# Turning the second norm's rows with VectorE and DRAM instead of TensorE, tile by tile, in a one-core transformer block

## The chip, the core and the metric

The kernel runs on one core of a Trainium2 chip. A core has five engines with a queue of instructions each, which run side by side and wait for each other through semaphores: TensorE (PE in the profile; its weight loads are PEld), VectorE (DVE), ScalarE (ACT), GpSimd (POOL) and SyncE (SP), which here issues nearly all the DMA transfers. [...] PSUM, where TensorE leaves its results, is used in eight banks of 128 rows by 512 f32 numbers. The metric is the device time of one execution in microseconds (us); the median of three runs before the change is 1670.11 us (1667.31 to 1671.17).

## The reference

One block with conditioning: a norm, attention with 32 query heads over one shared key and value head, a second norm, and two dense layers with ReLU. All is f32; x has 2048 rows of 512.

```python
mod = (_silu(c) @ w_mod).reshape(1, 6, 1, -1)
sa, ca, ga, sb, cb, gb = (mod[:, i] for i in range(6))
h = _layernorm(x) * (1 + ca) + sa
x = x + ga * attention(h)          # wq, wk, wv, wo; 32 heads of 16, one key/value head
h = _layernorm(x) * (1 + cb) + sb  # the second norm
x = x + gb * (relu(h @ w1) @ w2)   # 512 -> 1792 -> 512
```

The change concerns the second norm: its result `h` stands with rows of x on the partitions, and the first dense layer needs it turned, with the 512 features on the partitions.

## The kernel before, in words

The 2048 rows are worked in eight blocks of 256 (`TB`), each of two tiles of 128 rows (`TT`). After a start of some 115 us (first norm, keys, values, first queries) comes the main loop of 256 passes, called **steps** here: 32 steps to a block. A step has two parts, one per key tile of 128 keys. In a step TensorE computes 8 score tiles (`ps_exp`, L753, three banks), 8 tiles of scores for the row maxima of a later group of heads (`ps_max`, L426, three banks), and, at the end of each part, the products with the values (`ps_pv`, L879, one bank). ScalarE takes the exponential of each `ps_exp` tile (L755), VectorE the maximum over each `ps_max` tile (L428); each of them so gives a bank back to TensorE.

Between these, in a fixed order written as two strings (`PARTS`, a letter for each instruction or small group: c and d are scores, a and b maxima, u and l the two halves of other work), TensorE does other work from a generator: `behind(b)` hands out, one portion for each step, the output projection, second norm and dense layers of the block whose attention was finished last. A portion is mostly 6 or 12 products, each done as two halves of 64 rows (`on_half`, L163). The portions of a block are: steps 1 to 3 the rest of the second dense layer of the block before; steps 4 to 7 the output projection, two steps to each tile of 128 rows; steps 8 to 14 (`fill`) the second dense layer's second tile of the block before (in the first block of this kind: queries, and products that only keep TensorE busy); steps 15 to 28 the first dense layer; steps 29 to 32 the begin of the second. There are seven such blocks in the main loop; the eighth runs after it in `behind_last`, which the change does not touch.

The generator goes on by one portion inside the last l of a step (`advance`), and whatever it emits for the other engines on the way is written there, near the end of the step. Work in the list `put_off` is written a little into the next step, after the fourth letter of part one. The softmax sums of a group of heads come every eight steps (`normalise` at the end of steps 7, 15, 23 and 31, with a VectorE reciprocal, L789, and the transfers `recs` and `den` two steps later, and a product `on`, L923, on GpSimd one step after that).

The second norm in this setting: VectorE takes the sums of a tile (`ln_sums`: L208, L209), three small VectorE operations (L220 to L222) and thirteen small GpSimd ones (L230 to L235) give the reciprocal root (`ln_stats`), and three GpSimd passes over the tile make `xn` (`normed`: L482, L484, L485). TensorE then turns `xn` in two goes of four 128x128 squares (`turned_too`, in halves by `in_two`, L159), each go into a `ps_exp` bank that it takes from the scores; ScalarE copies that bank out (`stg`, L248) and `split` makes of it a high part (`hh`, ScalarE, L240) and a low part (`hl`, GpSimd, L241), which the first dense layer reads.

Of the kernel before, what the change touches and what calls it, by code (L numbers as in the profile page):

```python
# [19 lines left out]
P = 128  # L20
# [16 lines left out]

PARTS = "cbcuaucuautcuau", "tbldlbldlbldlad"  # L40
SYNC = mybir.DependencyInfo(mybir.DependencyClass.Sync, mybir.DependencyReason.DATA)
MANUAL = {ET.PE, ET.Activation, ET.DVE, ET.Pool, ET.SP}

# [13 lines left out]
def build(tc, nc, cst, sb, ps, dr, x, wq, wk, wv, wo, w1, w2, c, w_mod, out):  # L57
# [148 lines left out]
    def ln_sums(mv, t, src):  # L206
        st = sb.tile([P, 6], F32, name="st", tag="st", bufs=2)
        nc.vector.bn_stats(st, src)  # L208
        nc.vector.bn_aggr(mv[:, t], st)  # L209

    def ln_mv(n):
        return sb.tile([P, n, 2], F32, name="mv", tag="mv", bufs=2)
# [33 lines left out]
    def split_psum(hi, lo, pt, func=AF.Copy, stg=None, **kw):  # L246
        stg = stage() if stg is None else stg
        nc.scalar.activation(stg, pt, func, **kw)  # L248

        def parts():  # L250
            split(hi, lo, stg)

        return parts


    put_off = []

    def add_psum(dst, pt, other):
        stg = stage()
# [119 lines left out]
            qps[u].append(t.rearrange("p a n -> p (a n)"))  # L379


    later, turns = [], []

    negms = [cst.tile([P, 32], F32, name=f"negm{n}") for n in range(2)]
    for negm in negms:
# [69 lines left out]
    def turned(src, k2, pt):  # L455

        return [("turn", pt[:, (k * TT + t) * P:(k * TT + t + 1) * P],
                 src[:, t, (k2 * 2 + k) * P:(k2 * 2 + k + 1) * P])
                for k in range(2) for t in range(TT)]

    def flat(t, k2):
        return t[:, k2 * 2:k2 * 2 + 2].rearrange("p a n -> p (a n)")
# [17 lines left out]
    def normed(x1, xn, ts, nm, y, eng):  # L480
        for n, t in enumerate(ts):
            eng.tensor_scalar(xn[:, t], x1[:, t], nm[:, n:n + 1], y[:, n:n + 1],  # L482
                              op0=OP.add, op1=OP.mult)
            eng.tensor_tensor(xn[:, t], xn[:, t], cbr, op=OP.mult)  # L484
            eng.tensor_tensor(xn[:, t], xn[:, t], sbr, op=OP.add)  # L485
# [25 lines left out]
    def behind(b):  # L511
        def in_parts(todo, n):
            for i in range(0, len(todo), n):
                yield todo[i:i + n]

        def turned_too(src, parts, k2, bank):

            def turn():
                pt = bank()

                def end():
                    put_off.append(split_psum(flat(parts[0], k2), flat(parts[1], k2), pt))

                return turned(src, k2, pt), end

            turns.append(turn)

        def second(b, t):
            pt = ps_fill()
            yield from in_parts(dense2(b, t, pt), 6)  # L530
            ot = sb.tile([P, D], F32, name="ot", tag="tmp", bufs=2)
            add_psum(ot, pt, x1s[b][:, t])
            nc.sync.dma_start(out[b * TB + t * P:b * TB + (t + 1) * P], ot)

        x1, oo = open_block(b)
        if b == 0:
            qqs = [sb.tile([P, 2, LB], F32R, name="qq", tag="w1s", bufs=3) for _ in range(2)]
            rest, fill = [others_of(14 + n, qqs[n]) for n in range(2)]
            fill = itertools.chain(fill, [[]] * 4)
        else:  # L540
            rest, fill = carried.pop(), second(b - 1, 1)
        yield next(rest)
        yield next(rest)
        for k2 in range(DC // 2):
            put_off.append(partial(split, flat(oo[0], k2), flat(oo[1], k2), flat(on[b], k2)))
        yield from rest
        xn = sb.tile([P, TT, D], F32, name="xn", tag="xn", bufs=1)
        mv = ln_mv(TT)
        for t in range(TT):
            pt = ps_fill()  # L550
            for n, part in enumerate(in_parts(out_proj(pt, oo, t), 6)):
                yield part
                if t and n == 0:
                    ln_sums(mv, 0, x1[:, 0])
            add_psum(x1[:, t], pt, x1[:, t])
        ahead = [load_w1(f) for f in range(2)]

        def second_norm():
            ln_sums(mv, 1, x1[:, 1])
            stats = ln_stats(mv, TT, False)  # L560
            yield
            normed(x1, xn, range(TT), *stats, nc.gpsimd)
            yield

        norm2 = second_norm()
        hp = [sb.tile([P, DC, TB], F32R, name=n, tag="t4", bufs=2) for n in ("hh", "hl")]
        for n, part in enumerate(fill):
            if n in (4, 5):
                turned_too(xn, hp, n - 4, ps_exp)
            yield part  # L570
            next(norm2, None)
        r4 = r4s[b] = [sb.tile([P, 8, TB], F32R, name="r4", tag="big", bufs=4) for _ in range(4)]
        for f2 in range(FC // 2):
            pt = ps_fill()
            for f in range(f2 * 2, f2 * 2 + 2):
                if f + 2 < FC:
                    ahead.append(load_w1(f + 2))
                yield dense1(pt[:, (f % 2) * TB:(f % 2 + 1) * TB], ahead.pop(0), hp)
            i, f = divmod(f2 * 2, 8)
            put_off.append(split_psum(  # L580
                r4[i * 2][:, f:f + 2].rearrange("p a n -> p (a n)"),
                r4[i * 2 + 1][:, f:f + 2].rearrange("p a n -> p (a n)"), pt, AF.Relu))
        first_half = second(b, 0)
        yield from itertools.islice(first_half, 4)
        carried.append(first_half)
# [206 lines left out]

        return [back, partial(nc.gpsimd.tensor_tensor, on[b][:, g], num, den, op=OP.mult)]

    def in_two(turn):

        begun = []

        def first_part():
            begun.extend(turn())  # L800
            for d in begun[0]:
                on_half(d, 1)

        def second_part():
            for d in begun[0]:
                on_half(d, 0)
            begun[1]()

        return first_part, second_part

    def run(g):
        for _ in g:
            pass
# [59 lines left out]
    def values(s):  # L873
        nonlocal pvt
        u, kt = divmod(s, KT)
        if kt == 0:
            pvt = ps.tile([P, 512], F32, name="ps_pv", tag="pv", bufs=1)
        for i in range(4):
            nc.tensor.matmul(pvt[i * 32:(i + 1) * 32], vt[:, kt], pes.pop((s, i)),  # L879
                             start=(kt == 0), stop=(kt == KT - 1))  # L880
        if kt == KT - 1:

            ends.extend((s // 2 + 2 + n, end) for n, end in enumerate(normalise(u, pvt)))

    for c in range(NU * KT // 2):
        s = c * 2
        todo_of = dict(
            c=[partial(scores, *n) for n in ((s, 0), (s, 2), (s + 1, 0), (s + 1, 2))],
            d=[partial(scores, *n) for n in ((s + 2, 1), (s + 2, 3), (s + 3, 1), (s + 3, 3))
               if n[0] < NU * KT])  # L890
        if places:
            u, i, j = places.pop(0)
            todo_of.update(a=[partial(max_of, u, 0, i, j, kb) for kb in range(KB)],
                           b=[partial(max_of, u, 1, i, j, kb) for kb in range(KB)])
        for parts, load in later:
            put_off.append(parts)
            ends.append((c, load))
        later.clear()
        if not portion:

            pt = ps_fill()
            portion = [("f32r", pt, kp[:, 0:P], kp[:, 0:512], n == 0, n == 5) for n in range(6)]
        halves = [in_two(turn) for turn in turns]
        turns.clear()
        own = []
        for h in range(2):
            each = [partial(on_half, d, h) for d in portion]
            cuts = [len(each) * k // 6 for k in range(7)]
            own.append([partial(in_turn, each[x:y]) for x, y in zip(cuts, cuts[1:])])
        own[0].append(advance)  # L910
        todo_of.update(l=[partial(in_turn, own[0][k:k + 1 + k // 5]) for k in range(6)], u=own[1])
        for part in range(2):
            todo_of["t"] = [partial(in_turn, [half[part] for half in halves])]
            for n, what in enumerate(PARTS[part]):
                if todo_of.get(what):
                    todo_of[what].pop(0)()
                if part == 0 and n == 3:
                    in_turn(put_off)
                    put_off.clear()
            values(s + part)  # L920
        for due in [end for end in ends if end[0] <= c]:
            ends.remove(due)
            due[1]()  # L923
        next(todo, None)
        if c == NU * KT // 2 - 2:
            opened = open_last(NB - 1)
        if c and c % 32 == 0:
            assert next(others, None) is None
            others = behind(c // 32 - 1)
            portion = next(others)  # L930
# [31 lines left out]
```

## Time and profile before

| what | value |
|---|---|
| median of three runs | 1670.11 us |
| the profiled execution's own time | 1670.93 us |
| its span, first to last instruction | 1669.1 us |
| mean granted TensorE clock | 0.991 |
| busy: TensorE, VectorE, ScalarE, GpSimd | 98%, 81%, 74%, 21% of the span |
| products of the turns (L159) | 112, busy 12.3 us |

The page's first part gives the busy time of each engine as a share of the span. A matmul's end is modelled, so a busy TensorE can still wait. Steps can be read off the trace: a part of a step ends with the value products (`ps_pv`, L879), so the time from the start of one step's second group of them to the next step's is the length of one step. The view by windows gives the busy time of each engine, with the number of instructions in brackets, in stretches cut at these points. Of the seven blocks that run inside the loop, the one with steps 6 to 14 between 709.65 and 763.72 us is used for the timeline.

### The profile page before, as it was taken

The numbers are of one execution on the slowest core, as the hardware profiler recorded it, in microseconds if no ns is written. First come the engines' busy times: TensorE is split into PE (matmuls) and PEld (weight loads), VectorE is DVE, ScalarE is ACT, GpSimd is POOL, SyncE is SP. The second block draws the span as 40 slices with busy tenths as digits, with TensorE's granted clock in tenths as the row PEclk, the third lists the DMA queues.
The fourth block names the chain that finished last, engine by engine and source line by source line (L and its number), as shares of the span: only waits on it lengthen the run. The fifth ranks groups of instructions, "written<-read, shape, count | busy, mean of one in ns | idle before, by whom it ended". The sixth has DMA issues, their size and how long they took to land.

```text
span 1669.1 us, 34028 instructions
## 1 busy us (share of the span) xinstructions
PE 1644.1 (98%) x13130; PEld 927.4 (56%) x13130; DVE 1354.8 (81%) x2336; ACT 1228.9 (74%) x2399; POOL 345.3 (21%) x433
## 2 busy tenths in 40 slices
PE   7999999999999999999999999999999999999999
PEld 5445555555654566545654566546654565456668
DVE  7788888888888888888888888888889888888031
ACT  4228888877877788778877788778877788778831
POOL 3102355431101311131102211131103111131110
PEclk9699999999999999999999999999999999999999
DMA  8024643312311131112301131103311131103331
GB/s 285 23 73 121 206 133 104 92 62 68 115 29 48 34 110 63 35 42 86 105 17 48 47 104 55 54 23 99 92 30 36 50 115 40 61 17 101 116 115 57
DMA packets 88080, 129.86 MB, mean 78 GB/s; under 512 B 25140, under 2 KB 52724, under 8 KB 87920
## 3 DMA queue, kind: packets, MB, share of 16 engines
q1 hardware_dynamic: 86208, 127.55, 24.6%
q8 instruction: 105, 1.72, 0.4%
q14 instruction: 55, 0.45, 0.1%
q10 hardware_dynamic: 1712, 0.13, 0.1%
HBM read 100.33 MB, written 25.15 MB: 75 GB/s over the span
## 4 chain that ended last, share of the span: by engine, by line
PE 90%; ACT 4%; DVE 3%; issue 1%; DMA 1%; POOL 0%; SPq 0%; POOLq 0%; ACTq 0%; DVEq 0%
PE ps_pv L879 29%; PE ps_exp L753 21%; PE ps_max L426 18%; PE ps_fill L163 16%; ACT pe L755 3%; PE ps_exp L146 2%; PE ps_max L146 1%; DVE pm L428 1%; PE ps_exp L307 1%; PE ps_fill L146 1%; DVE st L208 1%; PE ps_exp L293 1%; DMA wmod<-in_w_mod_dram 1%; PE ps_exp L190 1%; PE ps_exp L159 0%
## 5 line engine op out<-in xcount | busy, mean ns | idle before, releaser
L428 DVE TENSOR_REDUCE pm<-ps_max 128x1 f32<-128x512 f32 x2048 | 1273.0, 682 | 189.6 <-PE ps_max L426 173.8
L755 ACT ACTIVATE pe<-ps_exp 128x512 f32<-128x512 f32 x2048 | 1081.9, 605 | 279.6 <-PE ps_fill L163 135.2
L426 PE MATMUL ps_max<-kp,qp 48*128 48x512 f32 x2048 | 848.8, 428 | 8.5 <-DVE pm L428 8.4
L753 PE MATMUL ps_exp<-qp,kp 50*128 50x512 f32 x2048 | 766.4, 415 | 3.7 <-ACT pe L755 2.0
L879 PE MATMUL ps_pv<-pe,vt 128*32 128x512 f32 x4096 | 545.5, 605 | 0.0
L426 PEld LDWEIGHTS ps_max<-kp,qp 48*128 48x128 f32 x2048 | 373.1, 186 | 269.1 <-DVE pm L428 234.3
L753 PEld LDWEIGHTS ps_exp<-qp,kp 50*128 50x128 f32 x2048 | 360.2, 185 | 266.1 <-ACT pe L755 176.9
L163 PE MATMUL ps_fill<-w2r,r 64*128 64x512 f32 x1044 | 289.2, 405 | 0.0
L163 PE MATMUL ps_fill<-hh,w1s 64*128 64x256 f32 x1568 | 229.1, 286 | 0.0
L163 PEld LDWEIGHTS ps_fill<-hh,w1s 64*128 64x128 f32 x1568 | 204.9, 186 | 6.7 <-PEq L156 6.7
L163 PEld LDWEIGHTS ps_fill<-w2r,r 64*128 64x128 f32 x1044 | 180.9, 185 | 7.6 <-PEq L156 2.5
L879 PEld LDWEIGHTS ps_pv<-pe,vt 128*32 128x32 f32 x4096 | 80.6, 108 | 128.0 <-issue 107.6
L241 POOL TENSOR_TENSOR r<-stg,r 128x512 fp32r<-128x512 f32 x49 | 62.9, 1284 | 317.5 <-ACT r L240 317.4
L163 PE MATMUL ps_fill<-hl,w1s 64*128 64x256 f32 x784 | 126.0, 280 | 0.0
L163 PE MATMUL ps_fill<-hT,wq 64*128 64x256 f32 x416 | 118.2, 399 | 0.0
L163 PEld LDWEIGHTS ps_fill<-hl,w1s 64*128 64x128 f32 x784 | 105.5, 186 | 0.0
L163 PEld LDWEIGHTS ps_fill<-hT,wq 64*128 64x128 f32 x416 | 70.1, 185 | 2.7
L923 POOL TENSOR_TENSOR on<-num,den 128x256 f32<-128x256 f32 x31 | 22.8, 736 | 230.0 <-DMA den<-recs 203.6
L769 POOL COPY num<-pvs 128x256 f32<-128x256 f32 x32 | 12.7, 397 | 174.9 <-ACT pvs L765 174.9
L241 POOL TENSOR_TENSOR hl<-stg,hh 128x512 fp32r<-128x512 f32 x14 | 17.9, 1282 | 128.0 <-ACT hh L240 128.0
L261 POOL TENSOR_TENSOR x<-stg,x 128x512 f32<-128x512 f32 x14 | 18.1, 1292 | 97.8 <-ACT stg L260 97.8
L248 ACT ACTIVATE stg<-ps_fill 128x512 f32<-128x512 f32 x62 | 38.1, 615 | 0.0
(147 smaller groups left out, 924.1 us busy)
## 6 DMA issues: line engine op xcount, KB each, us to landing
w1s<-w1dr SPq DMA_DIRECT2D x104, 512.0 KB
qdr<-qq SPq DMA_DIRECT2D x48, 256.0 KB
qp<-qdr SPq DMA_DIRECT2D x128, 96.0 KB
raw<-in_B_w_dram SPq DMA_DIRECT2D x28, 256.0 KB
w1dr<-w1s SPq DMA_DIRECT2D x14, 512.0 KB
wmod<-in_w_mod_dram SPq DMA_DIRECT2D x6, 1024.0 KB
x<-in_A_x_dram SPq DMA_DIRECT2D x8, 512.0 KB
out_dram<-ot SPq DMA_DIRECT2D x16, 256.0 KB
```

The source lines that it names most:

```text
L146: nc.tensor.matmul(pt, w, a, start=start, stop=stop)
L163: ins = nc.tensor.matmul(pt, w[r], a[r], start=start and h == 1, stop=stop and h == 0)
L190: nc.tensor.matmul(pt, sgw[:, k], wm[i][:, k], start=k == 0, stop=k == DC - 1)
L241: (eng or nc.gpsimd).tensor_tensor(lo, src, hi.bitcast(F32), op=OP.subtract)
L248: nc.scalar.activation(stg, pt, func, **kw)
L261: nc.gpsimd.tensor_tensor(dst, stg, other, op=OP.add)
L426: nc.tensor.matmul(pt, qps[u][i][r, j * P:(j + 1) * P], kp[r, kb * 512:(kb + 1) * 512], start=True, stop=True)
L428: nc.vector.tensor_reduce(pms[u][:, (i * 2 + hf) * 4 + j, kb:kb + 1], pt, axis=AX.X, op=OP.max)
L753: nc.tensor.matmul(pt, kp[r, kt * P:(kt + 1) * P], qps[u][ct // 2][r], start=True, stop=True)
L755: nc.scalar.activation(pe, pt, AF.Exp)
L879: nc.tensor.matmul(pvt[i * 32:(i + 1) * 32], vt[:, kt], pes.pop((s, i)), start=(kt == 0), stop=(kt == KT - 1))
L923: due[1]()
```

## The change

- The sums and statistics of the two tiles are kept apart (`mvs`, one each). The chain of the first tile (`norm_of(0)`) is written at step 8, before the sums of the second are taken; the second (`norm_of(1)`) at the end of step 9.
- TensorE's turns, their `ps_exp` banks and ScalarE's copies out of these are gone, with `turned_too`, `in_two`, `turns` and the letter t.
- Instead VectorE turns each tile of 128x512 in squares of 32 by 32 (`turn_of`: one STREAM_TRANSPOSE, into `xt`), for the first tile at the end of step 9, for the second in the second part of step 11 (`half_later`). Each `xt` is written to DRAM (`xdr`) by one transfer, so that four further transfers, written at the end of step 12, bring the squares back in their final places (`xh`, one transfer for each 32 partitions, in runs of 128 numbers).
- The splits of the two halves of `hh` and `hl` then read `xh` and stand together in step 14.

```diff
-PARTS = "cbcuaucuautcuau", "tbldlbldlbldlad"
+PARTS = "cbcuaucuaucuau", "bldlbldlbldlad"
...
         xn = sb.tile([P, TT, D], F32, name="xn", tag="xn", bufs=1)
-        mv = ln_mv(TT)
+        xdr = dr.tile([32, TT, 4, D], F32, name="xdr", tag="xdr", bufs=2)
+        mvs = [ln_mv(1) for t in range(TT)]
+
+        def norm_of(t):
+            normed(x1, xn, (t,), *ln_stats(mvs[t], 1, False), nc.gpsimd)
+
+        def turn_of(t):
+            xt = sb.tile([P, D], F32, name="xt", tag="tmp", bufs=2)
+            nc.vector.transpose(xt.rearrange("p (j k n) -> p k j n", j=4, k=DC),
+                                xn[:, t].rearrange("p (k j n) -> p k j n", j=4, k=DC))
+            nc.sync.dma_start(xdr[:, t].rearrange("a i n -> i a n"), xt)
+
...
         def second_norm():
-            ln_sums(mv, 1, x1[:, 1])
-            stats = ln_stats(mv, TT, False)
-            yield
-            normed(x1, xn, range(TT), *stats, nc.gpsimd)
+            put_off.append(partial(norm_of, 0))
+            yield
+            ln_sums(mvs[1], 0, x1[:, 1])
+            yield
+            norm_of(1)
+            turn_of(0)
+            yield
+            half_later.append(partial(turn_of, 1))
+            yield
+            yield
+            xh = sb.tile([P, TT * 4, DC, 32], F32, name="xh", tag="xn", bufs=1)
+            pieces = xdr.rearrange("a t i (j m) -> j a (t i) m", j=4)
+            for j in range(4):
+                nc.sync.dma_start(xh[j * 32:(j + 1) * 32].rearrange("p q k n -> p q (k n)"),
+                                  pieces[j])
+            yield
+            for k2 in range(DC // 2):
+                ks = slice(k2 * 2, k2 * 2 + 2)
+                put_off.append(partial(split, *[h[:, ks].rearrange("p k (q n) -> p k q n", n=32)
+                                                for h in hp],
+                                       xh.rearrange("p q k n -> p k q n")[:, ks]))
             yield
 
         norm2 = second_norm()
+        next(norm2)
         hp = [sb.tile([P, DC, TB], F32R, name=n, tag="t4", bufs=2) for n in ("hh", "hl")]
         for n, part in enumerate(fill):
-            if n in (4, 5):
-                turned_too(xn, hp, n - 4, ps_exp)
             yield part
             next(norm2, None)
...
-            todo_of["t"] = [partial(in_turn, [half[part] for half in halves])]
...
+                if part == 1 and n == 1:
+                    in_turn(half_later)
+                    half_later.clear()
```

On VectorE, steps 7 to 9 of a block: `st` and `mv` are the sums of a tile of `x`, `pm` the row maxima, of which a step has eight.

```order
 L208 BN_STATS st<-x_3717 128x6
 L209 BN_AGGR mv<-st 128x2
-L428 TENSOR_REDUCE pm<-ps_max 128x1 x16
+L428 TENSOR_REDUCE pm<-ps_max 128x1 x10
+L220 TENSOR_SCALAR ve<-mv 128x1
+L221 TENSOR_SCALAR y<-ve 128x1
+L222 TENSOR_SCALAR y<-y 128x1
+L428 TENSOR_REDUCE pm<-ps_max 128x1 x6
 L208 BN_STATS st<-x_3717 128x6
 L209 BN_AGGR mv<-st 128x2
-L220 TENSOR_SCALAR ve<-mv 128x2
-L221 TENSOR_SCALAR y<-ve 128x2
```

The three small operations of the first tile now stand between the sums of the two tiles, and none follow the second sums directly.

On VectorE, from step 9 to step 12, before the change (`negm` and `sq` are the maxima of a whole group of heads):

```order
L222 TENSOR_SCALAR y<-y 128x2
L428 TENSOR_REDUCE pm<-ps_max 128x1 x9
L789 RECIPROCAL rc<-rc 128x16
L428 TENSOR_REDUCE pm<-ps_max 128x1 x24
L432 TENSOR_REDUCE negm_156<-pm 128x16
L392 STREAM_TRANSPOSE sq<-negm_156 128x32
```

And the same stretch after it:

```order
L428 TENSOR_REDUCE pm<-ps_max 128x1 x8
L220 TENSOR_SCALAR ve<-mv 128x1
L221 TENSOR_SCALAR y<-ve 128x1
L222 TENSOR_SCALAR y<-y 128x1
L544 STREAM_TRANSPOSE xt<-xn 128x4x4x32
L428 TENSOR_REDUCE pm<-ps_max 128x1
L804 RECIPROCAL rc<-rc 128x16
L428 TENSOR_REDUCE pm<-ps_max 128x1 x13
L544 STREAM_TRANSPOSE xt<-xn 128x4x4x32
L428 TENSOR_REDUCE pm<-ps_max 128x1 x11
L432 TENSOR_REDUCE negm_156<-pm 128x16
L392 STREAM_TRANSPOSE sq<-negm_156 128x32
```

The second tile's three small operations, the first turn and the reciprocal now stand at one place with a single maximum between them; the second turn stands thirteen maxima later.

On TensorE, the middle of step 12 before the change (`ps_fill` is the other work):

```order
L426 MATMUL ps_max<-kp,qp 128x512
L163 MATMUL ps_fill<-w2r,r_4936 128x512
L159 MATMUL ps_exp<-idn,xn 128x64 x4
L753 MATMUL ps_exp<-qp,kp 128x512
L163 MATMUL ps_fill<-w2r,r_4936 128x512
L426 MATMUL ps_max<-kp,qp 128x512
L163 MATMUL ps_fill<-w2r,r_4937 128x512
L879 MATMUL ps_pv<-pe,vt 32x512 x4
L159 MATMUL ps_exp<-idn,xn 128x64 x4
```

In the changed program the two L159 rows are gone from this place and from the same place of step 13; the other rows keep their order.

On SyncE's queue, from the end of step 7 to step 13, after the change:

```order
L801 DMA rc<-sums 128x16
L546 DMA xdr<-xt 4x32x512
L805 DMA recs<-rc 128x16
L806 DMA den<-recs 128x1x256
L376 DMA qp<-qdr_3_127 48x2x256 x4
L546 DMA xdr<-xt 4x32x512
L571 DMA xh<-xdr 32x8x128 x4
L399 DMA mdr<-ms 16x2x32 x4
L405 DMA qp<-mdr 2x512 x4
```

The six `xdr` and `xh` rows are new; the others stood in this order before.

More of the change, by code (lines that the diff above doesn't have):

```diff
@@ L253, in split_psum @@
         return parts
-    put_off = []
+    put_off, half_later = [], []
     def add_psum(dst, pt, other):
@@ L379, in load_q @@
             qps[u].append(t.rearrange("p a n -> p (a n)"))
-    later, turns = [], []
+    later = []
     negms = [cst.tile([P, 32], F32, name=f"negm{n}") for n in range(2)]
@@ L514, in in_parts @@
                 yield todo[i:i + n]
[L516 to L526, printed above, removed]
         def second(b, t):
@@ L553, in behind @@
                 if t and n == 0:
-                    ln_sums(mv, 0, x1[:, 0])
+                    ln_sums(mvs[0], 0, x1[:, 0])
             add_psum(x1[:, t], pt, x1[:, t])
@@ L793, in normalise @@
         return [back, partial(nc.gpsimd.tensor_tensor, on[b][:, g], num, den, op=OP.mult)]
[L795 to L809, printed above, removed]
     def run(g):
@@ L902, in build @@
             portion = [("f32r", pt, kp[:, 0:P], kp[:, 0:512], n == 0, n == 5) for n in range(6)]
-        halves = [in_two(turn) for turn in turns]
-        turns.clear()
         own = []
```

## The prediction

> **What bounds the kernel now.** I read the page's busy shares and its chain of waits first.
>
> ```profile
> span 1669.1 us, 34028 instructions
> PE 1644.1 (98%) x13130; PEld 927.4 (56%) x13130; DVE 1354.8 (81%) x2336; ACT 1228.9 (74%) x2399; POOL 345.3 (21%) x433
> PE 90%; ACT 4%; DVE 3%; issue 1%; DMA 1%; POOL 0%; SPq 0%; POOLq 0%; ACTq 0%; DVEq 0%
> ```
>
> TensorE is on the chain for 90%. VectorE's mean of 81% says little; what counts is how much of it falls between two bank releases. So I cut one block at the start of the value products and took the view by windows, steps 6 to 13 (length first, then busy us and instructions of PE, PEld, DVE, ACT, POOL, then granted clock, DMA share, GB/s).
>
> ```profile
> 709.65:715.34 5.69, 5.69 (x47) 2.87 (x45) 4.96 (x9) 4.62 (x11) 1.29 (x1) 1.00 0.52 181
> 715.34:721.23 5.89, 5.89 (x46) 2.92 (x44) 5.63 (x11) 4.13 (x10) 0.00 (x0) 1.00 0.03 11
> 721.23:727.26 6.03, 5.94 (x46) 2.88 (x45) 4.97 (x9) 5.01 (x12) 1.64 (x2) 1.00 0.05 11
> 727.26:733.77 6.51, 6.06 (x46) 2.85 (x44) 6.15 (x14) 4.24 (x10) 3.54 (x15) 1.00 0.03 5
> 733.77:739.45 5.68, 5.68 (x46) 2.91 (x44) 5.13 (x10) 4.13 (x10) 5.44 (x5) 1.00 0.19 57
> 739.45:745.14 5.69, 5.69 (x46) 2.88 (x45) 4.96 (x9) 4.13 (x10) 0.99 (x2) 1.00 0.13 37
> 745.14:751.58 6.44, 6.44 (x54) 3.52 (x52) 5.31 (x9) 4.72 (x11) 0.00 (x0) 1.00 0.01 3
> 751.58:758.04 6.46, 6.46 (x54) 3.54 (x53) 5.50 (x11) 5.26 (x13) 1.49 (x2) 1.00 0.01 1
> ```
>
> An undisturbed step takes 5.68 us and leaves VectorE 5.68 - 4.96 = 0.72 us idle. Steps 12 and 13, with eight products more (54 against 46), are 0.76 and 0.78 us longer: these are the turns. Steps 7 and 9 are 0.21 and 0.83 us longer, and there VectorE does something besides maxima. Its timeline and the waits of step 9:
>
> ```profile
> 715.84 0.68 DVE L208 BATCH_NORM_STATS2 st<-x 128x6 f32<-128x512 f32 x1
> 716.55 0.18 DVE L209 BATCH_NORM_AGGREGATE mv<-st 128x2 f32<-128x6 f32 x1
> ...
> 727.75 0.68 DVE L208 BATCH_NORM_STATS2 st<-x 128x6 f32<-128x512 f32 x1
> ...
> 728.68 0.17 DVE L220 TENSOR_SCALAR ve<-mv 128x2 f32<-128x2 f32 x1
> ...
> 729.09 0.17 DVE L222 TENSOR_SCALAR y<-y 128x2 int32<-128x2 int32 x1
> ...
> 732.47 2.48 DVE L428 TENSOR_REDUCE pm<-ps_max 128x1 f32<-128x512 f32 x4 [0.22 <-PE ps_max L426]
> 734.87 0.24 DVE L789 RECIPROCAL rc<-rc 128x16 f32<-128x16 f32 x1
> ```
> ```profile
> PEld ps_max L426 <- DVE pm L428: 2.0, 3, 0.9
> ```
>
> This gives the price list of the whole prediction. A stretch of 0.90 us on VectorE (715.84 to 716.74) lengthens its step by 0.21; one of 1.51 us (727.75 to 729.26) by 0.83. In both, what passes 0.68 us is paid in full: the three `ps_max` banks cover the first 0.68 us, then TensorE waits for VectorE. The cover grows back at 0.72 us a step, so two stretches a step apart are priced one by one. The reciprocal in step 10 (0.24, with its gap 0.28) alone costs nothing.
>
> Over the seven blocks, sums of the same view over steps 12 and 13, step 9 and step 7, in this order:
>
> ```profile
> sum 90.31, PE 90.31 PEld 49.32 DVE 75.39 ACT 69.87 POOL 10.43; mean PE 12.90 PEld 7.05 DVE 10.77 ACT 9.98 POOL 1.49
> ```
> ```profile
> sum 45.81, PE 42.61 PEld 20.27 DVE 43.07 ACT 29.68 POOL 25.03; mean PE 6.09 PEld 2.90 DVE 6.15 ACT 4.24 POOL 3.58
> ```
> ```profile
> sum 41.24, PE 41.24 PEld 20.42 DVE 39.44 ACT 28.91 POOL 0.00; mean PE 5.89 PEld 2.92 DVE 5.63 ACT 4.13 POOL 0.00
> ```
>
> **The change, part by part.** *Turns off TensorE.* Steps 12 and 13 fall to what steps 10 and 11 are, with the same other work: 90.31 - 14 x 5.68 = 10.8 us gained. ScalarE's two copies out of the banks go with them, and the scores keep all three `ps_exp` banks; that lies in the same difference. At worst another wait takes the place and nothing is gained (a rival below).
>
> *Statistics apart.* The second sums now stand alone at the end of step 8, as the first do in step 7: step 9 falls to step 7's length, 45.81 - 41.24 = 4.6 us gained. The first tile's three small operations (728.68 to 729.26, with a gap 0.62 us) move into step 8. Cover: 0.68 us of banks, and the 0.34 us by which step 8 is longer while VectorE has only its maxima (4.97). I take 0; without the cover it would be 7 x 0.62 = 4.3 us. The cover then has some 4.5 us to grow back before the second sums, nearly enough.
>
> *The turn on VectorE.* No row shows a turn of 128x512. The nearest rows, and the ends:
>
> ```profile
> L392 DVE STREAM_TRANSPOSE sq<-negm 128x32 f32<-128x32 f32 x32 | 6.8, 212 | 3.6 <-DVE negm L432 0.5
> L428 DVE TENSOR_REDUCE pm<-ps_max 128x1 f32<-128x512 f32 x2048 | 1273.0, 682 | 189.6 <-PE ps_max L426 173.8 <-PE ps_fill L163 7.5 <-PE ps_exp L753 7.4
> L432 DVE TENSOR_REDUCE negm<-pm 128x16 f32<-128x64 f32 x32 | 7.0, 220 | 1.1
> L651 DVE TENSOR_SCALAR xn<-x,nm,y 128x512 f32<-128x512 f32 x1 | 0.5, 540 | 0.0
> L654 DVE TENSOR_TENSOR xn<-xn,sbr 128x512 f32<-128x512 f32 x1 | 1.7, 1676 | 0.0
> ```
>
> The same operation on 32 columns takes 212 ns. L428 against L432 prices a column at (682 - 220) / 448 = 1.03 ns, so 480 more make T = 0.212 + 0.495 = 0.71 us, which I take. Lower end: L651, 0.54. If the squares don't follow each other smoothly, each pays again what the one square costs above a small operation (212 - 170 = 42 ns): 0.17 + 16 x 0.042 = 0.84. Upper end: L654, 1.68, the slowest pass over 128x512 shown.
>
> First turn: at the end of step 9 stand 0.62 (small operations) + T + 0.05 (gap), one maximum, and the reciprocal's 0.28. The maximum between gives nothing back, so step 10 pays T + 0.95 - 0.68 = 0.98 us. Second turn: T + 0.05 - 0.68 = 0.08 us, in step 11. Together 1.06 x 7 = 7.4 us lost.
>
> *Does the turn wait?* VectorE would hold all its maxima behind it. GpSimd's rows:
>
> ```profile
> 723.54 0.39 POOL L769 COPY num<-pvs 128x256 f32<-128x256 f32 x1
> 728.74 0.22 POOL L230 TENSOR_SCALAR nm<-mv 128x2 f32<-128x2 f32 x1 [4.81 <-DVE mv L209]
> ...
> 734.93 1.29 POOL L485 TENSOR_TENSOR xn<-xn,sbr 128x512 f32<-128x512 f32 x1
> ```
>
> One tile's chain takes 736.22 - 728.74 = 7.5 us. The first now starts behind `num` at 723.9 and ends at 731.4. VectorE comes to its turn at 732.47 + 3 x 0.62 = 734.3, less the 0.62 that step 9 is shorter, plus the 0.62 of small operations: 734.3, so 2.9 us to spare. The second chain goes from y at 734.3 to 741.3 (7.0 us, as from 729.26 to 736.22); its turn comes after the first maximum of step 11's second part.
>
> ```profile
> 743.84 2.48 DVE L428 TENSOR_REDUCE pm<-ps_max 128x1 f32<-128x512 f32 x4 [0.33 <-PE ps_max L426]
> ```
>
> That is 744.5, moved by -0.62 + 0.98 to 744.8: 3.5 us to spare. The product `on` stays behind both chains, about 1 us later, and nothing in these steps reads it.
>
> *The transfers.* On SP the first `xdr` stands ahead of `recs` and `den`, which wait for a reciprocal that VectorE does after the turn anyway; they move by about 0.7 us. The second `xdr` and the four `xh` stand where SP is idle, ahead of `mdr`, whose turn comes some 6 us after the last of them (756.31 against 750.0, below).
>
> ```profile
> 736.61 0.66 SPq L791 DMA_DIRECT2D den<-recs  x1
> ...
> 756.31 1.70 SPq L399 DMA_DIRECT2D mdr<-ms  x4
> ```
> ```profile
> SPq L791 <- DMA recs<-rc: 1.1, 1, 1.1
> ```
> ```profile
> w1s<-w1dr SPq DMA_DIRECT2D x104, 512.0 KB
> ```
> ```profile
> 695.06 1.15 ACT L240 ACTIVATE oh<-on 128x512 fp32r<-128x512 f32 x2
> ```
> ```profile
> 692.56:698.26 5.70, 5.70 (x47) 2.88 (x45) 4.96 (x9) 5.16 (x12) 3.22 (x3) 1.00 0.12 36
> ```
>
> Turn done 745.6; issue 0.66 and landing 1.1 make 747.4; four issues end at 750.0. Two `w1s` loads of 512 KB fill 0.52 of step 6, so 1.5 us each; `xh` is as large but in runs of 512 bytes, for which I allow four times that: landed by 747.4 + 6 + 1.1 = 754.5. ScalarE reads it at step 14's start (758.04 + 0.36 + 0.08 - 1.54 = 756.9) plus 2.5, the place that `oh` has in step 3 (695.06 - 692.56): 759.4, so 4.9 us to spare. Its two splits standing together cost nothing: step 3 does the same pair in 5.70 us.
>
> *Sum:* -10.8 - 4.6 + 7.4 = -8.0 us. The profiled execution took 1670.93 us (span and 1.8 around it): 1662.9. The median of the runs shown is 0.8 lower; against it 1662.1.
>
> [...] The row says 212 ns for a turn of 128x32. [...] No run here shows 128 columns yet; the 212 ns are mostly the fixed part that the 170 ns operation beside it has too, and a price for each 128 columns counts that part four times.
>
> **The rivals.** *No change: the turn is priced by 128 columns.* If four pieces each pay the fixed part (4 x 212 ns = 0.85 us at the very least, 1.25 if each also takes its further 96 columns at 1.03 ns), then T = 1.25 and the turns cost 7 x (1.52 + 0.62) = 15.0 us: net -0.4, 1669.7 us. [...] Against it: it is one instruction, and L428's 512 columns show no such steps.
>
> *Slower: the turn is held up at VectorE's access to SBUF.* L654 took 1676 ns for the 512 columns that L651 passed in 540. If the turns, which read and write SBUF, take 1.68 while GpSimd works on the second chain, they cost 7 x (1.95 + 1.05) = 21.0 us: net +5.6, 1675.7 us. It decides from T = 1.28 on, where the loss reaches 15.4. Against it: L654 has two tensor inputs, and GpSimd is nearly idle at the second turn.
>
> *Slower: `xh` lands late.* From 4.9 us later than my bound, ScalarE holds its exponentials behind the split and TensorE soon follows; from 6.0 us the gain is gone; at 8 us later the loss is 7 x 3.1 = 21.7: net +13.7, 1683.8 us. Against it: the queue is idle there (shares of 0.13 and 0.01).
>
> *Slower: the 10.8 us don't come back,* because steps 12 and 13 meet another wait: -4.6 + 7.4 = +2.8, 1672.9 us. Against it: steps 10 and 11 do the same work in 5.68.
>
> **How the numbers follow.** About 0.2%, 3.3 us, is what a measurement here can tell from no change. Forecast, with T from 0.54 to 0.95: 0.78. By the same formula T = 0.54 gives -9.7 us (step 11 then pays nothing), 1660.4, T = 0.84 gives -6.2, 1663.9, and T = 0.95 -4.6, 1665.5. No change 0.08. Slower through SBUF 0.06, through late `xh` 0.04, through turns not regained 0.04. With 1 us for the spread of medians on the low side, and the space between forecast and no change half taken in on the high side, the range is 1659.4 to 1668.0. Faster 0.78, same 0.08, slower 0.14.
>
> **What would show it.** Right: steps 12 and 13 at 5.68 us with 46 products; step 9 near 5.89, step 10 near 6.66, step 11 under 5.85; L544 near 0.71 us without a GpSimd or DMA wait before it; `hh` in step 14 not waiting for `xh`. Wrong: L544 over 1.28 us; VectorE idle ahead of L544 with GpSimd as releaser; ScalarE idle in step 14 with `xh` as releaser; step 8 longer than 6.03.

## The result, and the profile after

The changed kernel takes 1658.7 us (median of 12 runs, 1652.43 to 1666.29) against 1667.24 us for the kernel before (median of 12 runs, 1658.81 to 1679.04): a ratio of 0.995, 95% interval 0.993 to 0.997, so 8.5 us by the medians (5.0 to 11.7 by the interval). The forecast was 8.0 us less, at 1662.1 us with a range from 1659.4 to 1668.0: the gain was met, the absolute time fell 0.7 us below the range. Why the one held and the other didn't is the subject of what follows.

The page of the changed kernel, span, busy times and chain:

```profile
span 1650.8 us, 33967 instructions
PE 1631.9 (99%) x13018; PEld 918.2 (56%) x13018; DVE 1359.6 (82%) x2371; ACT 1220.1 (74%) x2385; POOL 361.7 (22%) x524
PE 90%; ACT 4%; DVE 2%; DMA 1%; issue 1%; SPq 0%; POOL 0%; POOLq 0%; ACTq 0%; DVEq 0%
```

TensorE has 112 products fewer and is still the bound. The span is 18.3 us shorter than the one profiled before, more than twice the gain. Two windows of each kernel, the time up to the first value product and from there to the last, tell the parts of this; first the kernel before, then the changed one:

```profile
0.00:117.10 117.10, 104.58 (x386) 52.44 (x386) 89.73 (x198) 35.20 (x57) 21.13 (x35) 0.87 0.37 122
117.10:1599.88 1482.78, 1476.13 (x12389) 821.63 (x12387) 1245.13 (x2100) 1185.05 (x2328) 318.40 (x392) 1.00 0.24 73
```
```profile
0.00:106.55 106.55, 99.11 (x387) 51.00 (x387) 86.85 (x198) 35.09 (x57) 20.96 (x35) 0.94 0.41 134
106.55:1581.36 1474.81, 1469.43 (x12277) 813.87 (x12275) 1252.73 (x2135) 1176.34 (x2314) 335.01 (x483) 1.00 0.26 79
```

The main loop is 1482.78 - 1474.81 = 8.0 us shorter. The other 10.5 us lie in the start, which the change does not touch, at a granted clock (third number from the end) of 0.87 against 0.94: an estimate from these two clocks puts 0.13 x 117.10 - 0.06 x 106.55 = 8.8 us of them down to the clock.

Steps 7 to 14 of the same block as in the prediction, after the change:

```profile
703.90:709.80 5.90, 5.90 (x46) 2.91 (x44) 5.64 (x11) 4.13 (x10) 0.00 (x0) 1.00 0.01 3
709.80:715.81 6.01, 5.93 (x46) 2.88 (x44) 5.33 (x12) 5.01 (x12) 4.04 (x15) 1.00 0.05 11
715.81:721.71 5.90, 5.90 (x46) 2.90 (x45) 5.64 (x11) 4.13 (x10) 3.58 (x5) 1.00 0.02 3
721.71:727.95 6.24, 6.15 (x46) 2.89 (x44) 5.95 (x14) 4.18 (x10) 4.05 (x14) 1.00 0.15 33
727.95:733.63 5.68, 5.68 (x46) 2.88 (x44) 4.97 (x9) 4.13 (x10) 2.30 (x3) 1.00 0.35 105
733.63:739.33 5.70, 5.70 (x47) 2.94 (x45) 5.48 (x11) 4.14 (x10) 0.01 (x1) 1.00 0.19 47
739.33:745.02 5.69, 5.69 (x46) 2.94 (x45) 5.28 (x11) 4.24 (x11) 0.25 (x1) 1.00 0.35 97
745.02:750.70 5.68, 5.68 (x46) 2.88 (x45) 4.97 (x9) 5.14 (x12) 2.47 (x2) 1.00 0.02 4
```

Steps 12 and 13 are at 5.70 and 5.69 us, step 9 is at 5.90, step 10 at 6.24 (6.66 was expected), step 11 untouched. The turn's group, and VectorE's timeline at the first turn:

```profile
L544 DVE STREAM_TRANSPOSE xt<-xn 128x512 f32<-128x512 f32 x14 | 9.9, 706 | 0.0
```
```profile
722.20 0.14 DVE L220 TENSOR_SCALAR ve<-mv 128x1 f32<-128x1 f32 x1
722.38 0.15 DVE L221 TENSOR_SCALAR y<-ve 128x1 int32<-128x1 int32 x1
722.57 0.15 DVE L222 TENSOR_SCALAR y<-y 128x1 int32<-128x1 int32 x1
722.64 0.71 DVE L544 STREAM_TRANSPOSE xt<-xn 128x512 f32<-128x512 f32 x1
723.28 0.65 DVE L428 TENSOR_REDUCE pm<-ps_max 128x1 f32<-128x512 f32 x1
723.86 0.23 DVE L804 RECIPROCAL rc<-rc 128x16 f32<-128x16 f32 x1
724.01 1.22 DVE L428 TENSOR_REDUCE pm<-ps_max 128x1 f32<-128x512 f32 x2
```

A turn takes 706 ns, and VectorE never stood idle before one. The small operations, each of which reads what the one before wrote, stand 0.04 us apart; the turn and the maximum behind it, which read nothing of what stands just ahead of them, each start 0.07 to 0.08 us before the end of the operation ahead. So from the first small one to the next maximum are 1.08 us, where the prediction counted 1.38.

The sums of the view by windows over the seven blocks, changed kernel: steps 12 and 13, step 9, steps 10 and 11, and all of steps 7 to 14; below them steps 7 to 14 and steps 10 and 11 of the kernel before.

```profile
sum 79.99, PE 79.94 PEld 41.03 DVE 75.32 ACT 58.59 POOL 3.23; mean PE 11.42 PEld 5.86 DVE 10.76 ACT 8.37 POOL 0.46
...
sum 41.47, PE 41.47 PEld 20.55 DVE 39.47 ACT 28.94 POOL 24.98; mean PE 5.92 PEld 2.94 DVE 5.64 ACT 4.13 POOL 3.57
...
sum 83.73, PE 83.14 PEld 40.46 DVE 76.45 ACT 59.15 POOL 44.35; mean PE 11.88 PEld 5.78 DVE 10.92 ACT 8.45 POOL 6.34
...
sum 330.15, PE 327.61 PEld 162.94 DVE 303.47 ACT 246.65 POOL 118.07; mean PE 46.80 PEld 23.28 DVE 43.35 ACT 35.24 POOL 16.87
```
```profile
sum 338.87, PE 335.07 PEld 171.05 DVE 296.19 ACT 254.84 POOL 101.93; mean PE 47.87 PEld 24.44 DVE 42.31 ACT 36.41 POOL 14.56
...
sum 79.63, PE 79.63 PEld 40.57 DVE 70.66 ACT 58.85 POOL 46.06; mean PE 11.38 PEld 5.80 DVE 10.09 ACT 8.41 POOL 6.58
```

338.87 - 330.15 = 8.7 us come from these eight steps; the rest of the loop is 0.7 us longer, about what two traces of one kernel differ by (0.6, below). One thing in them was not forecast: in the first of the seven blocks ScalarE waits in step 14 for the transfers (the view of waits, ScalarE, that step), and the step takes 7.52 us.

```profile
ACT hh L240 <- DMA xh<-xdr: 1.8, 1, 1.8
```
```profile
375.10:382.62 7.52, 6.20 (x46) 2.76 (x44) 5.58 (x10) 5.15 (x12) 2.38 (x2) 1.00 0.23 63
```

SyncE's own waits in steps 10 to 13 of the block above say where the transfers lose time:

```profile
SPq L571 <- DMA xdr<-xt: 5.4, 1, 5.4
SPq L806 <- DMA recs<-rc: 5.0, 1, 5.0
```

The write of a turned tile lands 5.4 us after it was issued, and `recs`, 8 KB behind the first such write, 5.0 us instead of the 1.1 of before.

### The profile page after: what moved, and what is told of

Read it like the earlier page. It is cut to its first block, busy times and chain, and to the rows that moved or that the text cites. A ratio compares the mean times of both kernels' runs of the same rounds, so it can differ in the third digit from the quotient of the medians.

```text
span 1650.8 us, 33967 instructions
## 1 busy us (share of the span) xinstructions
PE 1631.9 (99%) x13018; PEld 918.2 (56%) x13018; DVE 1359.6 (82%) x2371; ACT 1220.1 (74%) x2385; POOL 361.7 (22%) x524
## 4 chain that ended last, share of the span: by engine, by line
PE 90%; ACT 4%; DVE 2%; DMA 1%; issue 1%; SPq 0%; POOL 0%; POOLq 0%; ACTq 0%; DVEq 0%
PE ps_pv L878 29%; PE ps_exp L768 21%; PE ps_max L426 18%; PE ps_fill L163 16%; ACT pe L770 3%; PE ps_exp L146 2%; PE ps_max L146 1%; DVE pm L428 1%; PE ps_fill L146 1%; PE ps_exp L307 1%; PE ps_exp L190 1%; DMA wmod<-in_w_mod_dram 0%; DMA xdr<-xt 0%; PE ps_exp L293 0%; PE ps_fill L190 0%
```

## The experiments

The theory: each stretch of extra VectorE work at one place is covered by the `ps_max` banks up to 0.60 us, counted from its start to the start of the next maximum (0.81 us cost 0.21 in step 7, 1.42 cost 0.83 in step 9 before), and paid in full beyond that. The main rival: the turn is dear by itself, or VectorE's total work sets the price.

### Statistics alone

The kernel before, with the tiles' statistics apart and TensorE's turns kept.

```diff
-            ln_sums(mv, 1, x1[:, 1])
-            stats = ln_stats(mv, TT, False)
+            put_off.append(partial(norm_of, 0))
             yield
-            normed(x1, xn, range(TT), *stats, nc.gpsimd)
+            ln_sums(mvs[1], 0, x1[:, 1])
+            yield
+            norm_of(1)
             yield
```

> Only the statistics are taken tile by tile; TensorE keeps its turns. Theory (each stretch of extra VectorE work at one place is free up to a cover of 0.60 us and paid in full beyond it): step 9 falls from 6.51 to 5.89 us, step 10 stays at 5.68 because its 0.44 us of small operations and the reciprocal stay under the cover, steps 12 and 13 stay at 6.45: 7 x -0.62 = -4.3 us against the kernel before, ratio about 0.9974. Rival (the price is the total of VectorE's work in the block, wherever it stands): no change, since the work is only moved.

Measured: ratio 0.9959 (0.9936 to 0.9981). Steps 9 and 10 together take 11.59 us instead of 6.51 + 5.68 = 12.19 in a block:

```profile
721.90:733.49 11.59, 11.59 (x91) 5.82 (x89) 10.98 (x23) 8.26 (x18) 7.06 (x19) 1.00 0.08 23
```

So 0.60 us a block come back by moving work that is as long as before; VectorE's total does not set the price. Small operations and reciprocal together are free, as the theory has it, and steps 12 and 13, where TensorE keeps its turns, stay at 6.45 us each. The loop as a whole was only 2.5 us shorter than in the profile of before: one step, the third of the first block, took 1.25 us more, as ScalarE waited 1.3 us there for GpSimd's product `on`. At this size the steps are the better measure.

### No turn at all

The changed kernel without VectorE's turns and without the six transfers (the splits read `xn` as it stands, so the dense layer's rows are not turned).

```diff
             norm_of(1)
-            turn_of(0)
...
-            half_later.append(partial(turn_of, 1))
```

> The changed kernel without any turn: VectorE's turns and the six transfers are left out, and the splits read xn unturned, so the first dense layer gets unturned rows. Theory: step 10 falls from 6.25 to 5.68 us and step 14 of the first block loses its 1.85 us: 7 x 0.57 + 1.85 = 5.9 us less inside the loop than the changed kernel; nothing else moves. Rival (the transfers slow other work down all over the block): more than 7 us less, with steps 11 to 14 of the later blocks shorter too.

Measured in one run of 1655.89 us, the loop and step 10 of one block:

```profile
116.57:1584.84 1468.27, 1464.83 (x12277) 814.66 (x12275) 1244.78 (x2121) 1176.39 (x2314) 334.95 (x483) 1.00 0.24 74
728.54:734.23 5.69, 5.69 (x47) 2.93 (x45) 5.34 (x13) 4.12 (x10) 3.50 (x14) 1.00 0.05 10
```

Step 14 of the first block is at 5.69 us too. Steps 11 to 14 of the later blocks lie within 0.03 us of the changed kernel's, but for step 13 of the fourth (5.69 against 6.00). The loop is 6.5 us shorter, where 5.9 were expected. So the change pays 0.57 us a block for the turn, nearly all of it in step 10, and 1.8 us once for late transfers; of the 0.7 us left, 0.3 are that step 13.

### The first turn half a step later

```diff
             norm_of(1)
-            turn_of(0)
+            half_later.append(partial(turn_of, 0))
```

> The first tile's turn stands in the second part of step 10 instead of the end of step 9, away from the small operations and the reciprocal. Theory of the cover: step 10 pays nothing at its start (0.44 + 0.15 us under 0.60) and about 0.2 us at the turn, as the cover has then grown back by only some 0.4 us: step 10 about 5.85 instead of 6.25 us, 7 x -0.4 = -2.8 us against the changed kernel, about -11 us against the kernel before (ratio 0.9933). Rival (the turn itself is dear at that moment, for its access to SBUF or because the first transfer starts): step 10 stays near 6.25 and nothing is gained.

Measured: ratio to the kernel before 0.9914 (0.9883 to 0.9945). Step 10 takes 5.69 us and step 11 5.70: the turn, with the same 0.70 us and the same transfers, costs 0.04 where it had cost 0.57. The rival falls. Step 10 of one block, and VectorE ahead of the turn in it:

```profile
722.47:728.17 5.70, 5.70 (x47) 2.94 (x45) 5.35 (x13) 4.13 (x10) 3.50 (x14) 1.00 0.04 6
```
```profile
726.86 0.69 DVE L428 TENSOR_REDUCE pm<-ps_max 128x1 f32<-128x512 f32 x1 [0.28 <-PE ps_max L426]
727.46 0.70 DVE L544 STREAM_TRANSPOSE xt<-xn 128x512 f32<-128x512 f32 x1
```

The theory's size was off the other way: the cover had grown back nearly whole within half a step, not to 0.4 us. VectorE had caught up by then, since one maximum ahead of the turn it stood idle for 0.28 us, waiting for TensorE's scores. But step 12 of the first block went from 5.71 to 9.29 us:

```profile
363.22:372.51 9.29, 7.95 (x46) 3.35 (x44) 6.22 (x11) 4.45 (x10) 0.00 (x0) 0.82 0.38 128
```
```profile
DVE xt L544 <- DMA xdr<-xt: 2.1, 1, 2.1
```
```profile
364.00:367.00 3.00, 1.66 (x12) 0.78 (x8) 2.29 (x4) 1.19 (x3) 0.00 (x0) 1.00 0.52 173
367.00:370.00 3.00, 3.00 (x18) 1.03 (x14) 2.62 (x5) 1.42 (x3) 0.00 (x0) 0.53 0.36 115
```

VectorE waited 2.1 us for the first tile's write before the second turn, TensorE stood still behind it, and then had its clock halved for some 3 us (0.53 in the second window); the step is 3.6 us longer, for a wait of 2.1.

### Other buffers for the turned tiles

The same kernel with the turned tiles in a pool of three buffers.

```diff
-            xt = sb.tile([P, D], F32, name="xt", tag="tmp", bufs=2)
+            xt = sb.tile([P, D], F32, name="xt", tag="stg", bufs=3)
```

> As with the later first turn, but the turned tiles stand in buffers of a pool of three in place of one of two. Theory (in the first block the second turn waited 2.1 us for the first tile's slow write, because a buffer in between was taken by the query work and the second turn got the first one's buffer; TensorE then ran at half clock for 3.4 us): step 12 of the first block falls from 9.29 to about 5.7 us and the clock stays full there; its step 14 may wait for the late transfers again, by up to 2 us. Rival (the wait is for something else of the first block): step 12 stays near 9.3.

Measured in one run of 1648.42 us (the kernel before beside it: 1665.99), first block's steps 12 and 14:

```profile
364.60:370.29 5.69, 5.69 (x47) 2.93 (x45) 5.47 (x10) 4.13 (x10) 0.00 (x0) 1.00 0.49 163
```
```profile
375.96:382.89 6.93, 6.20 (x47) 2.79 (x45) 5.59 (x10) 5.17 (x12) 2.38 (x2) 1.00 0.24 65
```

As the theory said: the wait was for the buffer, the clock stays full without it, and the late transfers show again in step 14.

### The DRAM tile in the order of the partitions

```diff
-        xdr = dr.tile([32, TT, 4, D], F32, name="xdr", tag="xdr", bufs=2)
+        xdr = dr.tile([TT, 4, 32, D], F32, name="xdr", tag="xdr", bufs=2)
...
-            nc.sync.dma_start(xdr[:, t].rearrange("a i n -> i a n"), xt)
+            nc.sync.dma_start(xdr[t].rearrange("i a n -> (i a) n"), xt)
...
-            pieces = xdr.rearrange("a t i (j m) -> j a (t i) m", j=4)
+            pieces = xdr.rearrange("t i a (j m) -> j a (t i) m", j=4)
```

> The tile in DRAM is laid out in the order of the partitions, so that a write to it is one plain pattern of 128 rows instead of 4 by 32. Theory (the pattern with an outer size of 4 is spread over few of the 16 DMA engines: 128 packets of 0.13 us took 4.3 us): the write lands in under 2.5 us instead of 5.4, the wait of den on recs behind it falls from 5.0 to under 2.5 us, and in the first block step 14 falls from 7.5 to 5.68 us: 1.9 us less than the changed kernel. Rival (the write to DRAM takes 5 us whatever its pattern): no difference anywhere.

Measured: ratio 0.9934 (0.9908 to 0.996); step 14 of the first block 5.68 us; loop 1473.1 us, 1.7 less than the changed kernel. The ratio alone could not be told from the changed kernel's 0.995. SyncE's waits in steps 10 to 12:

```profile
SPq L571 <- DMA xdr<-xt: 1.7, 1, 1.7
SPq L806 <- DMA recs<-rc: 1.3, 1, 1.3
```

The same 256 KB in the same 2 KB pieces land after 1.7 us instead of 5.4, and `recs` is nearly back at its old 1.1 us. That the write with an outer size of 4 keeps few of the 16 DMA engines busy agrees with the changed kernel's trace: in the four microseconds in which its second write is the only transfer under way, the DMA share (last but one) is 0.24, or 3.8 engines of 16. For the write in the order of the partitions there is only the fall from 5.4 to 1.7 us.

```profile
735.00:739.00 4.00, 4.00 (x35) 2.37 (x32) 3.78 (x7) 2.82 (x6) 0.00 (x0) 1.00 0.24 60
```

### Each turn twice

```diff
-            nc.vector.transpose(xt.rearrange("p (j k n) -> p k j n", j=4, k=DC),
-                                xn[:, t].rearrange("p (k j n) -> p k j n", j=4, k=DC))
+            for _ in range(2):
+                nc.vector.transpose(xt.rearrange("p (j k n) -> p k j n", j=4, k=DC),
+                                    xn[:, t].rearrange("p (k j n) -> p k j n", j=4, k=DC))
```

> Each of VectorE's two turns is done twice in a row. Theory of the cover: each further turn is paid in full, 0.63 us from start to start: step 10 grows from 6.25 to 6.88 us, step 11 from 5.68 to 1.26 - 0.60 = 0.66 more, 6.34: 7 x 1.29 = 9.0 us more than the changed kernel, so about level with the kernel before (+0.5 us). Rival (VectorE has slack over the block, 0.72 us a step, and catches up): under 5 us more.

Measured: ratio to the kernel before 1.0015 (0.9988 to 1.0042); the loop takes 1484.1 us, 9.3 more than the changed kernel (9.0 expected). Steps 10 and 12 of one block:

```profile
731.14:738.14 7.00, 6.16 (x46) 2.88 (x44) 6.67 (x15) 4.24 (x10) 4.72 (x15) 1.00 0.13 30
```
```profile
743.83:750.27 6.44, 6.44 (x46) 2.99 (x45) 6.19 (x11) 4.34 (x10) 0.00 (x0) 1.00 0.16 41
```

Each further turn costs 0.75 us, slightly over its own length, and the second tile's shows one half step later than I had said, in step 12. VectorE does not catch up over the block. This also prices the prediction's rival of a turn slowed at SBUF: at twice the turn's length the whole gain is gone.

### Both improvements together

The later first turn and the DRAM order together.

> The later first turn and the DRAM layout in the order of the partitions together. Theory: the two gains add up, 2.8 + 1.9 us less than the changed kernel, some 13 us less than the kernel before (ratio 0.992); step 10 about 5.85 us, step 14 of the first block 5.68. Rival (the later turn makes its transfer late and eats the gain): step 13 or 14 longer than 5.8.

Measured: 1652.43 us (median of 6 runs) against 1666.3 (16 runs), ratio 0.9907 (0.9874 to 0.994). Step 10 takes 5.68 us, step 12 of the first block 5.69 and its step 14 5.71. Start and loop:

```profile
0.00:113.19 113.19, 103.60 (x387) 53.39 (x387) 89.06 (x198) 35.12 (x57) 21.02 (x35) 0.89 0.39 126
113.19:1581.64 1468.45, 1464.95 (x12277) 814.97 (x12275) 1251.98 (x2135) 1176.50 (x2314) 334.89 (x483) 1.00 0.26 79
```

The loop's 1468.45 us equal the 1468.3 of the kernel without any turn: nothing of the turn's price is left. Of the kernels that turn the tiles this one has the shortest loop, 14.3 us shorter than before and 6.4 shorter than with the change as it was made.

### The kernel before once more

> The kernel before once more, for a second trace of it. Theory (single runs differ because TensorE's clock is granted at half speed for some stretches of the first 120 us, and the main loop always takes the same time): the loop from the first value product to the last takes 1485.6 us within 1 us, and the time to the first value product differs from 117.1 with the time at half clock. Rival (the runs differ all over the span): the loop differs by more than 2 us.

Measured in one run of 1671.17 us:

```profile
0.00:116.72 116.72, 104.28 (x386) 52.31 (x387) 89.52 (x198) 35.18 (x57) 20.94 (x35) 0.88 0.37 122
116.72:1600.12 1483.40, 1476.71 (x12388) 822.27 (x12387) 1246.13 (x2100) 1184.84 (x2328) 318.20 (x392) 1.00 0.24 73
```

The loop, by the same cut, takes 1483.40 us against 1482.78: within 1 us of each other (the 1485.6 of the expectation was cut a little later). The start is long again, at a clock of 0.88. In four of the traces shown the start takes 106.55, 113.19, 116.72 and 117.10 us at clocks of 0.94, 0.89, 0.88 and 0.87. The kernel before is not slower there by its code: the kernel without any turn, whose start is that of the changed kernel, takes 116.57 us for it. Over the changed kernel's 12 runs the fastest, 1652.43 us, has a mean granted clock of 0.996 and the slowest, 1666.29, one of 0.988; 0.008 of 1660 us are 13.3, nearly the whole spread of 13.9.

## Why the prediction was right, and where it was wrong

**The sum.** By the seven blocks' windows:

| term | predicted, us | measured, us |
|---|---|---|
| turns off TensorE (steps 12, 13) | -10.8 | 90.31 - 79.99: -10.3 |
| statistics apart (step 9) | -4.6 | 45.81 - 41.47: -4.3 |
| turns on VectorE (steps 10, 11) | +7.4 | 83.73 - 79.63: +4.1 |
| late transfers (first block, step 14) | 0 | 7.52 - 5.68: +1.8 |
| steps 7 to 14 in all | -8.0 | -8.7 |

The three mechanisms are shown. With the statistics alone, step 9 falls and steps 12 and 13 stay at 6.45 us; with TensorE's turns gone too, these fall to 5.68 and 5.69; the turn left out or done twice moves step 10 by about what the price list says. Of the 0.5 us missing in the first row, 0.3 are step 13 of the fourth block (below, under what is open).

**What was wrong: the absolute time.** The step that failed is "The median of the runs shown is 0.8 lower; against it 1662.1", with the "1 us for the spread of medians on the low side". Three runs had given 1670.11 us; twelve gave 1667.24, 2.9 lower, and the same -8.0 from there is 1659.2, which by itself lies under the range. Further runs of the kernel before, beside the experiments, bear the lower base out: medians of 1667.67 (25 runs) and 1666.3 (16 runs). The spread was visible in the material: three runs from 1667.31 to 1671.17, and a start with its granted clock well below 1 in the profiled one. The measured ratio of 0.995 is what the sum gives (1 - 8.0 / 1667.24 = 0.9952).

**What was mis-sized: the first turn, 0.98 us, measured 0.57.** T itself was right (0.71 predicted, 0.706 measured). Too large was the company it was counted in: small operations of one column take 0.15 instead of 0.17 us, the turn and the maximum behind it start before the operation ahead has ended, and the reciprocal moved the next maximum by 0.15 (723.86 to 724.01), not 0.28. From start to start the stretch is 1.08 + 0.15 = 1.23, less the cover, which is 0.60 and not 0.68 by the same count: 0.63. The second turn's 0.08 was 0.03 by this count (0.63 from 732.93 to 733.56 in the trace); step 11 shows none of it, and step 12 0.01 to 0.03. That the cover "grows back at 0.72 us a step" also fell: the later first turn shows it back within half a step.

**What was mis-sized the other way: the transfers.** "Issue 0.66 and landing 1.1" took the landing from an 8 KB transfer; the 256 KB write took 5.4 us. The 4.9 us to spare were gone in the first block, where three query transfers (`qdr`) stand ahead in SyncE's queue and the second write took 7.4 us, and step 14 waited 1.8 us. That was the rival of late transfers, in one block of seven. The "four times" allowed for `xh` in runs of 512 bytes was my own estimate, which no run bears out: in the block shown its 512 KB moved within 4 us (DMA shares of 0.58, 0.72, 0.59 and 0.13 in the microseconds from 741 to 745), where 6 + 1.1 were allowed. The errors, 3.3 us too dear here, 1.8 us too cheap there and 0.8 us too hopeful in the first two rows, largely cancelled, so that the sum came out right is in part luck.

**Rivals.** The turn priced by 128 columns (1.25 us by the rows) and the hold-up at SBUF (1.68 us) did not come: all fourteen turns lie between 0.70 and 0.71 us. In this place eight turns on TensorE cost 1.5 us of a bound engine (10.3 over the seven blocks), while VectorE's two operations cost 0.57, and nothing where they are placed well (a loop of 1468.45 us against 1468.3 without any turn). Nor did another wait take the place of TensorE's turns, as steps 12 and 13 are at 5.70 and 5.69 us. Step 8, where 0.62 us of small operations were costed at nothing, stayed at 6.01 us.

**Open.** Step 13 of the fourth block is 0.31 us longer in four of the six kernels with transfers and in none without. In each of the four VectorE stands idle for 0.46 us ahead of its transpose `sq` there, where 0.11 is usual; in the changed kernel:

```profile
925.15 0.21 DVE L392 STREAM_TRANSPOSE sq<-negm 128x32 f32<-128x32 f32 x1 [0.46 <-DVE negm L432]
```

The kernel before, which has none of these transfers, has the same wait of 0.46 us once (at 1123.97), in a step that is no longer than the same step of its other blocks. So the transfers need not be the cause; what `sq` waits for is not shown.

## What to carry to other kernels

Here VectorE's work, which gives three `ps_max` banks back to TensorE, was priced by place, not by amount: extra work up to the banks' cover of 0.60 us was free, so that the first turn cost 0.04 us half a step later where it had cost 0.57 in a row with the small operations and the reciprocal. The count that came nearest is from start to start (1.23 - 0.60 = 0.63). So place extra pieces apart. Try a large outermost dimension for a slow transfer: the write with 4 there landed after 5.4 us, the same bytes with 128 after 1.7. Take a landing time from a transfer of its own shape: the 1.1 us of 8 KB were no measure for the 256 KB that took 5.4. And when effects of half a per cent are forecast, forecast the difference (8.0 us forecast, 8.5 measured), and read from the granted clock how far the base itself moves (0.988 to 0.996 over the changed kernel's 12 runs, 13.9 us apart).

## What the runs showed of the hardware that was not expected

One wait of 2.1 us cost more than itself. In the kernel with the later first turn TensorE stood still for 1.34 us in step 12 of the first block, and the 3.41 us behind the stretch that holds this standstill ran at half clock (0.50); the step lost 3.6 us for the wait of 2.1:

```profile
363.76:367.17 3.41, 2.07 (x16) 0.78 (x8) 2.46 (x5) 1.60 (x3) 0.00 (x0) 1.00 0.51 173
367.17:370.58 3.41, 3.41 (x16) 1.03 (x14) 2.45 (x5) 1.25 (x3) 0.00 (x0) 0.50 0.34 108
```

With each turn done twice the first block's step 10 took 8.76 us, at a clock of 0.81, against 7.00 in the others. The length of the standstill does not decide it alone. That step stands still for 0.85 us, and the same step of the second block for 0.81 at full clock; the 7.52 us step of the changed kernel stands still for 1.32 and keeps its full clock too. What does decide is not shown.
